# One written order for the whole first half: attention, W, a*b and c of batch 0

## The chip, the cores and the metric

The kernel runs on one core of a Trainium2 chip. The metric is the time of one execution on the device in microseconds (us). TensorE (PE) does the matmuls, ScalarE (ACT) and VectorE (DVE) read PSUM and do elementwise work, GpSimd (POOL) does elementwise work from SBUF to SBUF, and SyncE (SP) issues every DMA. Each of these engines works through its own list of instructions in order.

## The reference, cut to what matters

Attention over 16 heads of 576 tokens (two batches of eight heads), then two feed-forward parts:

```
scores = q @ k^T / 8, causal; a = softmax(scores); local = a @ v
q_p = phi(q); mem_out = (q_p @ M_prev) / (q_p @ z_prev + 1e-6)
attn = g * mem_out + (1 - g) * local          # g from beta, per head

x = attn, heads side by side                  # 1152 tokens x 512
h = (x @ w1) * (x @ w2) @ w3;  x = h @ w_out  # w3: 1024x1024, w_out: 1024x512
p = probs / sum(probs)
out = sum over 4 experts e of p[:, e] * (relu(x @ ew1[e]) @ ew2[e])
```

The weights `w1`, `w2`, `w3`, `w_out` arrive as 64-bit floats.

## The kernel before, in words

Heads are worked on in eight pairs: 0 to 3 are batch 0, 4 to 7 batch 1. Each matrix is split into a rounded high part and a low remainder, and a product is three matmuls (`PASSES`): high by low, low by high, high by high.

The first half of the program has four kinds of work:

- **Attention**, pair by pair. The parts are named by letters, a pair number and sometimes a step: `hq`, `hk`, `lq`, `lk` split q and k; `e`, `f` make phi; `s` scores (PE), `m` mask and row minimum (DVE), `x` exponential (ACT); `t` transposes (PE) and `c` their copies (ACT); `n`, `g` the memory read; `v` probabilities by v (PE), `j` and `ja` join the results (DVE, POOL); `z`, `zh`, `zl` write the transposed result `xT` (PE, ACT, DVE).
- **W = w3 @ w_out**, formed once, in 16 units of `u`: `wa` (ACT) and `wd` (DVE) turn a tile of 64-bit numbers into 32-bit ones, `wp` splits it on POOL, `w{u}_0` to `w{u}_3` are 12 matmuls into a bank `wacc`, and `y` takes the sum out: units 0 to 7 into `half` by ACT, units 8 to 15 added to `half` on DVE as `both`, which is then split into `W`. The eight tiles of `w_out` come by `oa`, `od`, `oh`, `ol` into `wo`.
- **a*b of batch 0**: 16 units, alternately of w1 and w2. Each is loaded, turned (ACT, DVE), written back to DRAM as `wf` for batch 1, split on POOL into `ws`, and gives two products `ab` of 12 matmuls. The products of the even unit are copied (`asb`, ACT), those of the odd one multiplied into it (DVE), and the result is split into `hT` (ACT, DVE).
- **c of batch 0** = W by hT: eight banks of 24 matmuls, each copied out by ACT into `x2`.

After these come a*b and c of batch 1 and the expert stage, about 462 us of the span.

A list of names, `FIRST`, states the order of PE, ACT, DVE and POOL for pairs 0 to 3 and units 0 to 6 of W, inside a `manual_schedule` block. Everything behind it is placed by rules: `run_slot` merges the steps of one pair with a share of `fill` work by fractions (`A_AT`, `T_AT` and so on; W's units in slot 4, a*b in slots 5 and 6, c in slot 7), and the Tile scheduler then decides the order of the instructions on each engine. SP's order is decided by the scheduler throughout.

Raw weight tiles are loaded ahead through `staging`: the first `RING` loads go to four slots in `main`, those behind them to two slots of the tag `raw`, where a load waits until the join two loads earlier has read its slot (`ahead`, `fetch`). In `FIRST` these loads are of `wo` and `w3`; a*b's loads have code of their own in `BUnits`.

Of the kernel before, what the change touches and what calls it, by code (L numbers as in the profile page):

```python
# [8 lines left out]
F32 = mybir.dt.float32  # L9
# [37 lines left out]
def kernel(  # L47
# [117 lines left out]
    def load_pair(p):  # L165

        ts = []
        for nm, src in (("q", qT), ("k", kT)):
            t = A2.tile([P, src.shape[-1]], F32, tag=f"{nm}d", name=f"{nm}d{p}")
            nc.sync.dma_start(out=t, in_=src[p])  # L170
            ts.append(t)
        raw_t[p] = ts
# [7 lines left out]
    def named(fs, ats):  # L180
        parts.update(fs)
        return [*zip(ats, fs.values())]

    def stage_h(p):

        if p >= B * H // 2:
            return []
        qd, kd = raw_t[p]

        def split(i):  # L190
            if p not in qk_t:
                qk_t[p] = [A1.tile([P, 2, w], F32R, tag=f"{x}s", name=f"{x}s{p}") for x, w in (("q", S + SB), ("k", S))]
            return (qk_t[p][i], (qd[:, 0 : S + SB], kd)[i])
# [8 lines left out]

        return named({f"hq{p}": lambda: hi(0), f"hk{p}": lambda: hi(1), f"lq{p}": lambda: lo(0), f"lk{p}": lambda: lo(1)}, H_AT)

    def stage_phi(p):

        if p >= B * H // 2:
            return []
        qd = raw_t[p][0][:, P:]
        st = {}  # L210

        def f0():
            st["ex"] = ex = A1.tile([P, S], F32, tag="ex", name=f"ex{p}")
            nc.scalar.activation(ex, qd, AF.Exp)

        def f1():
# [3 lines left out]
            nc.vector.scalar_tensor_tensor(out=phi, in0=qd, scalar=0.0, in1=ex, op0=ALU.max, op1=ALU.add)  # L220

        return named({f"e{p}": f0, f"f{p}": f1}, PHI_AT)

    def stage_a(p):

        if p >= B * H // 2:
            return []
        banks = {}
        prob_t[p] = Pt = {}
        mn = A2.tile([P, NS2 + 1], F32, tag="mn", name=f"mn{p}")  # L230
# [48 lines left out]
        return [(at, lambda c=c: (scores(*c), peaks(c))) for at, c in zip(A_AT, steps)]  # L279
# [13 lines left out]
    def stage_b(p):  # L293
# [5 lines left out]
        def trans(g):  # L299
# [16 lines left out]
            return lambda: (f(), copy())  # L316
# [85 lines left out]
        def fin_lo():  # L402
# [6 lines left out]
        return [  # L409
            *zip(T_AT, (trans(g) for g in range(len(GROUPS)))),  # L410
            (MEM_AT, lambda: (mem(), mem_out())), (PV_AT[0], pv(0)), (PV_AT[1], lambda: (pv(1)(), pv_last())),
            (JOIN_AT, lambda: (join(), join_mem())), (FIN_AT, lambda: (fin(), fin_hi(), fin_lo())),
        ]

    def run_slot(n, fill):
        steps = stage_h(n + 2) + stage_phi(n + 1) + stage_a(n + 1)
        steps += stage_b(n) if n >= 0 else []
        steps += [((i + 0.5) / len(fill), f) for i, f in enumerate(fill)]
        for _, f in sorted(steps, key=lambda t: t[0]):
            f()  # L420

# [21 lines left out]
    def wo_unit(c):  # L443
# [22 lines left out]
    def w_conv(u):  # L466
# [14 lines left out]
        fs = {f"wa{u}": acts, f"wd{u}": join, f"wp{u}": split}  # L481
        parts.update(fs)
        return lambda: [f() for f in fs.values()]

    def w_mm(u, c):
# [8 lines left out]
        if c == 3 and u >= W_FIRST:  # L494
            w_out_of(u)

    def w_out_of(u):
        g, t = divmod(u, KF)
        if g == 0:
            nc.scalar.copy(half[t], wacc[u])  # L500
        else:
            both = pf.tile([P, DM], F32, tag="asb", name=f"both{t}", bufs=1)
# [5 lines left out]
    def w_unit(u):  # L508
        def post():
            if u + 2 < NU:  # L510
                w_conv(u + 2)()

        return [lambda c=c: w_mm(u, c) for c in range(4)] + [post]

# [5 lines left out]
    class BUnits:  # L520


        def __init__(self, b, hi, lo):
            self.b, self.pool, self.hi, self.lo, self.ahead = b, pf, hi, lo, 2 + 2 * b
            self.raw, self.ws, self.asb = {}, {}, {}

        def load(self, u):
# [7 lines left out]
            self.raw[u] = r = self.pool.tile([P, KD, P, 2], U32, tag="raw", name=f"wr{self.b}_{u}")  # L535
# [15 lines left out]
        def mm(self, u, a):  # L551
            b = self.b
            m, w = divmod(u, 2)
            ps = psM.tile([P, 512], F32, tag=f"M{a}", name=f"ab{b}_{u}_{a}", bufs=1)
# [8 lines left out]
            if w == 0:  # L563
                if a == 0:
# [514 lines left out]
```

## Time and profile before

| | us |
|---|---|
| median of 3 runs | 720.12 (718.15 to 721.86) |
| the profiled execution's own time | 721.79 |
| its span, first to last instruction | 720.0 |
| PE busy | 691.7 (96%) |
| DVE busy | 423.6 (59%) |
| ACT busy | 375.7 (52%) |
| POOL busy | 368.5 (51%) |

Busy time of PE holds the time of matmuls that overlap, and a matmul is shown longer than its share of the stream. So a busy PE is not yet a PE at its best pace; that is read from chains of matmuls that follow each other without a wait. The span was profiled once; the profiled execution took 1.8 us more than its span.

### The profile page before, as it was taken

How to read it: one execution, taken by the hardware profiler on the slowest of the kernel's cores; microseconds unless marked ns; L12 is line 12 of the kernel's file. 1: busy time of each engine (PE TensorE's matmuls, PEld its weight loads, DVE VectorE, ACT ScalarE, POOL GpSimd, SP SyncE). 2: the span in 40 equal slices, each digit the busy share in tenths (PEclk: the TensorE clock that was granted, in tenths of full speed). 3: DMA queues.
4: the chain of work that ended last, by engine and by line, in shares of the span. 5: the costliest groups of instructions: out<-in, count | busy, mean ns of one | idle time of the engine just before them, and what ended most of it. 6: DMA issues, size and time to landing. Idle time of an engine off the chain costs nothing.

```text
span 720.0 us, 12876 instructions
## 1 busy us (share of the span) xinstructions
PE 691.7 (96%) x4952; PEld 616.7 (86%) x4952; DVE 423.6 (59%) x785; ACT 375.7 (52%) x793; POOL 368.5 (51%) x357
## 2 busy tenths in 40 slices
PE   4889998989999999999999999999999999999997
PEld 3667775779899999999898999889999989998896
DVE  6698899877743133335866565346554455634563
ACT  6879967465733143336454554454554455444441
POOL 3435546637341050002776776566866577766660
PEclk9999999999999999999999999999999999999999
DMA  8663333354530022102212331313231313221511
GB/s 285 229 196 127 99 116 117 120 193 150 176 133 30 9 100 69 60 17 71 90 59 66 111 118 59 117 59 104 73 117 59 117 60 117 91 86 59 188 31 59
DMA packets 43404, 74.53 MB, mean 104 GB/s; under 512 B 14416, under 2 KB 14416, under 8 KB 43344
## 3 DMA queue, kind: packets, MB, share of 16 engines
q1 hardware_dynamic: 43344, 73.72, 30.7%
q8 instruction: 39, 0.64, 0.4%
q14 instruction: 21, 0.17, 0.1%
HBM read 67.15 MB, written 6.55 MB: 102 GB/s over the span
## 4 chain that ended last, share of the span: by engine, by line
PE 77%; DVE 10%; ACT 4%; DMA 4%; POOL 2%; issue 2%; SPq 0%; DVEq 0%; ACTq 0%
PE o L905 27%; PE Z L952 14%; PE ab L558 11%; PE Q L952 7%; PE c L665 6%; PE R L952 3%; PE a L331 2%; PE wacc L490 2%; PE pt L307 2%; PE sc L252 1%; DMA qd<-in_q_cols_dram 1%; DMA wr<-in_moe_w_tiles_dram 1%; PE sc L240 1%; DVE tf_l L126 1%; DMA wor<-in_moe_w_out_dram 1%
## 5 line engine op out<-in xcount | busy, mean ns | idle before, releaser
L905 PE MATMUL o<-w,he 128*128 128x512 f32 x864 | 224.0, 392 | 0.0
L93 POOL TENSOR_TENSOR w<-r,w 128x512 fp32r<-128x512 f32 x96 | 129.8, 1352 | 165.1 <-ACT w L786 159.8
L905 PEld LDWEIGHTS o<-w,he 128*128 128x128 f32 x864 | 153.7, 188 | 23.8
L558 PE MATMUL ab<-xT,ws 128*128 128x288 f32 x768 | 111.1, 298 | 3.4 <-DVE asb L652 1.9
L558 PEld LDWEIGHTS ab<-xT,ws 128*128 128x128 f32 x768 | 103.4, 188 | 6.5 <-issue 2.0
L890 ACT ACTIVATE he<-t 128x320 fp32r<-128x320 f32 (+1 forms) x96 | 42.7, 445 | 118.3 <-DVE t L981 70.5
L891 DVE SCALAR_TENSOR_TENSOR he<-t,he 128x320 fp32r<-128x320 f32 (+1 forms) x96 | 57.8, 602 | 49.1 <-ACT he L890 49.1
L96 DVE TENSOR_TENSOR w<-r,w 128x512 fp32r<-128x512 f32 x64 | 66.7, 1044 | 0.0
L974 DVE TENSOR_TENSOR t<-u,Q 128x320 f32<-128x320 f32 (+1 forms) x32 | 14.5, 454 | 82.4 <-ACT u L972 82.4
L786 ACT CAST w<-r 128x512 fp32r<-128x512 f32 x96 | 58.9, 614 | 4.4 <-POOL r L799 2.6
L490 PE MATMUL wacc<-wo,w3s 128*128 128x512 f32 x192 | 54.1, 419 | 3.1 <-DVE both L503 2.7
L665 PE MATMUL c<-hT,W 128*128 128x288 f32 (+2 forms) x384 | 53.9, 296 | 0.0
L665 PEld LDWEIGHTS c<-hT,W 128*128 128x128 f32 x384 | 51.7, 188 | 0.3
L952 PE MATMUL Z<-X0T,w 128*128 128x320 f32 x288 | 50.3, 310 | 0.1
L952 PEld LDWEIGHTS Z<-X0T,w 128*128 128x128 f32 x288 | 46.1, 188 | 4.1 <-ACT u L968 0.6
L490 PEld LDWEIGHTS wacc<-wo,w3s 128*128 128x128 f32 x192 | 35.2, 195 | 12.9 <-issue 5.1
L952 PEld LDWEIGHTS Z<-X1T,w 128*128 128x128 f32 x288 | 41.0, 188 | 4.0
L952 PE MATMUL Z<-X1T,w 128*128 128x256 f32 x288 | 42.1, 282 | 0.0
L816 ACT CAST w<-r 128x512 fp32r<-128x512 f32 x64 | 39.5, 618 | 0.0
L266 DVE CUSTOM_DVE_ANT_0 P<-sc,mask 128x128 f32<-128x128 f32 (+4 forms) x72 | 33.7, 513 | 8.6 <-PE sc L240 5.7
L271 ACT ACTIVATE P<-P,mn 128x128 f32<-128x128 f32 (+4 forms) x72 | 37.5, 582 | 2.2 <-DVE mn L266 2.2
L793 POOL TENSOR_TENSOR t<-r 128x256 f32<-128x256 f32 x32 | 32.1, 1003 | 7.9 <-DMA r<-in_moe_w_tiles_dram 7.9
(131 smaller groups left out, 1175.9 us busy)
## 6 DMA issues: line engine op xcount, KB each, us to landing
r<-in_moe_w_tiles_dram SPq DMA_DIRECT2D x64, 256.0 KB, 3.7
r<-in_moe_w_dram SPq DMA_DIRECT2D x64, 256.0 KB, 2.9
w3r<-in_moe_w_tiles_dram SPq DMA_DIRECT2D x16, 512.0 KB, 3.9
wr<-in_moe_w_tiles_dram SPq DMA_DIRECT2D x16, 512.0 KB, 3.6
wor<-in_moe_w_out_dram SPq DMA_DIRECT2D x8, 512.0 KB, 5.5
wf<-tf SPq DMA_DIRECT2D x16, 256.0 KB, 2.1
wr<-wf SPq DMA_DIRECT2D x16, 256.0 KB, 2.8
qd<-in_q_cols_dram SPq DMA_DIRECT2D x8, 352.0 KB, 3.1
```

Of the source, the lines that this page charges most:

```text
L93: nc.gpsimd.tensor_sub(dst, src, r32(hi))
L96: nc.vector.tensor_sub(dst, src, r32(hi))
L271: nc.scalar.activation(Pt[i, x], Pt[i, x], AF.Exp, bias=one, scale=-1.0)
L490: nc.tensor.matmul(wacc[u], lhsT=w3s[u][:, a, c, :], rhs=wo[4 * g + c][:, bb, :], start=(c == 0 and x == 0), stop=(c == 3 and x == 2),)
L558: nc.tensor.matmul(ps[:, 0:HS], lhsT=self.ws[u][:, wi, kk, :], rhs=xT[b, kk][:, xi, a * HS : (a + 1) * HS], start=(n == 0), stop=(n == 3 * ...
L665: nc.tensor.matmul(st["ps"], lhsT=Wt[kk][:, wi, d * P : (d + 1) * P], rhs=hT[kk][:, xi, t0 : t0 + tw], start=(kk == 0 and x == 0), stop=(k ...
L786: return lambda: nc.scalar.copy(st["w"][i][:, 0], src(i))
L816: return lambda: nc.scalar.copy(w2s[s][x][:, 0], st["r"][:, x])
L890: nc.scalar.activation(h[:, 0], src, AF.Relu)
L891: nc.vector.scalar_tensor_tensor(out=h[:, 1], in0=src, scalar=0.0, in1=r32(h[:, 0]), op0=ALU.max, op1=ALU.subtract)
L905: nc.tensor.matmul(o_ps[i], lhsT=h_of[s][x][:, a, i * P : (i + 1) * P], rhs=w2s[s][x][:, b, :], start=first, stop=last,)
L952: nc.tensor.matmul(ps, lhsT=w1s[s][a][:, wi, kk, :], rhs=X[c, b][:, xi, kk, :], start=first and kk == 0 and x == 0, stop=(kk == 1 and x == ...
```

## The change: what it does

`FIRST` now holds 720 names and states the order for all eight pairs, all of W, a*b of batch 0 and c of batch 0, in one `manual_schedule` block. `run_slot`, the fractions, `spread` and `fills` are gone. The functions that made several steps at once (`w_unit`, `w_out_of`, `emit`, `BUnits.unit` for batch 0) are cut into named parts, so that each can be placed. a*b's loads of batch 0 go through `staging` and the same chain of loads as `wo` and `w3`, `RING` is 12 instead of 17, and q and k of a pair are loaded apart. W's units 7 to 15 stood in pair 4's slot; in the list, a*b's units 0 to 7 come between W's first half and its second, and units 8 to 15 behind W. The number of matmuls and of elementwise instructions stays as it was. Batch 1 and the expert stage are written as before and are still placed by the scheduler.

```diff
-FIRST_PAIRS, W_FIRST, RING = 4, 7, 17
-W_SLOTS, B_SLOTS, C_SLOTS = (4.0, 5.0), (5.0, 7.0), (7.0, 8.0)
+zl3 s40 y4 s41 wp6 oa4 m40 w5_0 w5_1 m41 x40 w5_2 od4 w5_3 x41 w6_0 wp7 y5 w6_1 ba0 w6_2 w6_3 oh4 bd0 w7_0 y6 w7_1 ol4
...
+b5_1 rm20 bp6 rh20 v51 rm21 rh21 rl20 b6_0 bd7 rl21 wa8 b6_1 bp7 bc60 v52 head14 head15 bc61 wd8 b7_0 j5 wa9 wp8 b7_1
...
+RING = 12
-    def load_pair(p):
...
+    def load(nm, p):
+        src = {"q": qT, "k": kT}[nm]
+        raw_t[nm, p] = t = A2.tile([P, src.shape[-1]], F32, tag=f"{nm}d", name=f"{nm}d{p}")
+        nc.sync.dma_start(out=t, in_=src[p])
...
-    def run_slot(n, fill):
...
-        if c == 3 and u >= W_FIRST:
-            w_out_of(u)
...
+    def w_sum(u):
+        def add():
+            if g == 0:
+                nc.scalar.copy(half[t], wacc[u])
+                return
+            st["f"] = both = pf.tile([P, DM], F32, tag="asb", name=f"both{t}", bufs=1)
             nc.vector.tensor_add(both, half[t], wacc[u])
+        def hi():
             Wt[t] = main.tile([P, 2, DM], F32R, tag=f"u{t}", name=f"W{t}")
-            nc.scalar.copy(Wt[t][:, 0, :], both)
-            lo_dve(Wt[t][:, 1, :], both, Wt[t][:, 0, :])
+            nc.scalar.copy(Wt[t][:, 0, :], st["f"])
...
-            self.raw[u] = r = self.pool.tile([P, KD, P, 2], U32, tag="raw", name=f"wr{self.b}_{u}")
+            self.raw[u] = r = staging(f"wr{self.b}_{u}")
...
+        def acts(self, u):
+            self.raw[u] = from64_acts(self.raw[u], self.pool, f"0_{u}")
+        def join(self, u):
+            self.raw[u] = f = from64_join(*self.raw[u])
+            wf[u] = wd.tile([P, KD, P], F32, tag=f"f{u}", name=f"wf{u}")
+            nc.sync.dma_start(out=wf[u], in_=f)
+            ahead()
...
+        def keep(self, u, a):
+            nc.scalar.copy(self.asb[m][:, a, :], self.ps[u, a][:, 0:HS])
+        def times(self, m, a):
+            nc.vector.tensor_mul(pa_, self.ps[2 * m + 1, a][:, 0:HS], pa_)
+        def h_hi(self, m, a):
+            nc.scalar.copy(hT[m][:, 0, a * HS : (a + 1) * HS], self.asb[m][:, a, :])
+        def h_lo(self, m, a):
+            lo_dve(hT[m][:, 1, sl], self.asb[m][:, a, :], hT[m][:, 0, sl])
...
-    order = [f for f in FIRST if f[:2] in ("oa", "wa")]
-    order += [f"wa{u}" for u in range(W_FIRST + 2, NU)]
+    order = [f for f in FIRST if f[:2] in ("oa", "wa", "ba")]
...
-    fills = spread(W_SLOTS, [w_unit(u) for u in range(W_FIRST, NU)])
-    fills += [(B_SLOTS[0], [b0_start])] + spread(B_SLOTS, [b0.unit(u) for u in range(NU)])
-    fills += [(7.5, [b1.start])]
-    fills += spread(C_SLOTS, [c_unit(0, d, a * HS, HS, ps_main(d, a)) for d in range(KD) for a in range(2)])
...
+    with tc.manual_schedule(engines=ENGINES):
+        for f in FIRST:
+            parts[f]()
+    b1.start()
```

In the new list `ba`, `bd`, `bp` are acts, join and split of a unit of a*b, `b{u}_0` and `b{u}_1` its products, `bc` the copy, `rm`, `rh`, `rl` the product and its split, `k` and `kc` the matmuls and copies of c.

On PE, this is where W's second half begins before, beside pair 4 (`sc_5` are scores of pair 5, `pt_4` transposes of pair 4; the numbers behind the last `_` only tell tiles apart):

```order
L490 MATMUL wacc_1481<-wo_123,w3s_1389 128x512 x3
L490 MATMUL wacc_1481<-wo_124,w3s_1389 128x512 x3
L490 MATMUL wacc_1481<-wo_125,w3s_1389 128x512 x3
L252 MATMUL sc_5_1438<-ks_1254,qs_1253 128x128 x6
L252 MATMUL sc_5_1438<-ks_1254,qs_1253 128x256 x5
L490 MATMUL wacc_1406<-wo_126,w3s_1322 128x512 x3
L252 MATMUL sc_5_1438<-ks_1254,qs_1253 128x256
L307 MATMUL pt_4_1485<-identF,P_8_1273 64x128
L252 MATMUL sc_5_1492<-ks_1254,qs_1253 128x384 x6
L490 MATMUL wacc_1481<-wo_126,w3s_1389 128x512 x3
```

Units 8 (`wacc_1406`) and 9 (`wacc_1481`) stand in pieces between each other and between single matmuls of the scores. After the change PE's list reads there, with `ab_7` unit 7 of a*b and `sc_6` the scores of pair 6:

```order
L536 MATMUL ab_7_1_2044<-xT_3_74,ws_7_1995 128x288 x3
L467 MATMUL wacc_2064<-wo_123,w3s_2041 128x512 x3
L467 MATMUL wacc_2064<-wo_124,w3s_2041 128x512 x3
L467 MATMUL wacc_2064<-wo_125,w3s_2041 128x512 x3
L467 MATMUL wacc_2064<-wo_126,w3s_2041 128x512 x3
L244 MATMUL sc_6_2087<-ks_1724,qs_1723 128x384 x6
L244 MATMUL sc_6_2094<-ks_1724,qs_1723 128x512 x6
L467 MATMUL wacc_2105<-wo_123,w3s_2076 128x512 x3
```

Units, products and score steps stand whole, and unit 8 has moved behind a*b's unit 7.

On DVE, this is what stands ahead of the first addition of W's second half (`both`) before; `ex_2209` and `ex_2756` are phi of pairs 6 and 7, `tf_l` the joins of later w3 tiles:

```order
L219 TENSOR_SCALAR ex_2209<-ex_2209 128x576
L126 SCALAR_TENSOR_TENSOR tf_l_1470<-tf_l_1470,tu_l_1471 128x512
L127 SCALAR_TENSOR_TENSOR tf_l_1470<-w3r_1216,tf_l_1470 128x512
L220 SCALAR_TENSOR_TENSOR phi_2251<-qd_1341,ex_2209 128x576
L126 SCALAR_TENSOR_TENSOR tf_l_1516<-tf_l_1516,tu_l_1517 128x512
L219 TENSOR_SCALAR ex_2756<-ex_2756 128x576
L127 SCALAR_TENSOR_TENSOR tf_l_1516<-w3r_1387,tf_l_1516 128x512
L126 SCALAR_TENSOR_TENSOR tf_l_1589<-tf_l_1589,tu_l_1590 128x512
L127 SCALAR_TENSOR_TENSOR tf_l_1589<-w3r_1476,tf_l_1589 128x512
L503 TENSOR_TENSOR both_1433<-half_63,wacc_1406 128x512
```

After the change the addition of the same unit stands between two mask steps of pair 6 (`P_12`, `P_13`; `mn` rows read their minimum), behind one w3 join and the last a*b rows:

```order
L134 SCALAR_TENSOR_TENSOR tf_l_2079<-tf_l_2079,tu_l_2080 128x512
L135 SCALAR_TENSOR_TENSOR tf_l_2079<-w3r_2015,tf_l_2079 128x512
L105 TENSOR_TENSOR hT_3_2058<-asb_3_1998,hT_3_2058 128x288
L260 ISA P_12_2117,mn_1836<-sc_6_2094,mask 128x512
L260 ISA P_13_2119,mn_1836<-sc_6_2094,mask 128x512
L481 TENSOR_TENSOR both_2130<-half_63,wacc_2064 128x512
L260 ISA P_12_2134,mn_1836<-sc_6_2087,mask 128x384
L260 ISA P_13_2136,mn_1836<-sc_6_2087,mask 128x384
```

No phi of later pairs and no more than one w3 join stand directly ahead of it.

## Rows read from the trace of the kernel before

**Rows 1.** Busy us of each engine by stretch; clock, DMA.
```profile
0.00:80.00 80.00, 64.78 (x661) 50.25 (x663) 62.83 (x159) 64.80 (x126) 34.04 (x38) 0.98 0.62 203
80.00:258.00 178.00, 171.20 (x1512) 148.84 (x1511) 117.27 (x235) 95.85 (x188) 78.36 (x68) 0.99 0.34 114
75.00:136.00 61.00, 56.78 (x475) 43.98 (x475) 53.84 (x107) 43.15 (x80) 33.26 (x27) 0.97 0.32 104
100.00:120.00 20.00, 15.86 (x92) 10.62 (x92) 18.68 (x41) 14.55 (x28) 7.68 (x7) 0.91 0.35 123
258.00:270.00 12.00, 10.93 (x81) 10.50 (x80) 6.00 (x8) 5.73 (x13) 6.21 (x6) 1.00 0.23 74
```
**Rows 2.** PE's waits, 80 to 270 us: total, times, longest.
```profile
PE wacc L490 <- DVE both L503: 2.7, 1, 2.7
```
**Rows 3.** The chain that ended last, 94 to 120 us: start, us, what.
```profile
96.05 4.46 DMA qd<-in_q_cols_dram
...
112.32 0.61 DVE both L503
...
115.42 3.99 PE wacc L490 x11
```
**Rows 4.** The chain, 76 to 90 us, where PE never waits.
```profile
76.79 0.72 PE sc L252 x6
...
78.52 1.37 PE wacc L490 x6
79.89 1.32 PE a L331 x40
81.21 0.91 PE sc L252 x6
...
84.33 0.88 PE a L341 x20
85.20 1.00 PE sc L240 x6
...
87.58 0.87 PE pt L307 x8
88.45 0.90 PE b L365 x8
89.34 0.29 PE b L369 x4
```
**Rows 5.** The chain, 188 to 250 us: products of a*b, transposes back.
```profile
188.39 1.58 PE ab L558 x12
190.95 1.79 PE ab L558 x12
...
249.59 0.44 PE x L392 x4
250.03 0.29 PE x L397 x4
```
**Rows 6.** Busy us of c's matmuls alone, 80 to 258 us: PE, PEld, ACT.
```profile
80.00:258.00 178.00, 26.27 (x191) 25.50 (x192) 2.79 (x7) 0.99 0.34 114
```
**Rows 7.** Groups by line: a*b's turning, then w3's join at 75 to 136 us.
```profile
L119 ACT ACTIVATE tu<-wr 128x512 uint32<-128x512 uint16 x14 | 9.5, 679 | 17.0 <-DMA wr<-in_moe_w_tiles_dram 15.9 <-DVE mn L266 0.6 <-DVE tf L126 0.3
L126 DVE SCALAR_TENSOR_TENSOR tf<-tf,tu 128x512 uint32<-128x512 uint32 x16 | 13.9, 871 | 7.6 <-ACT tf L120 7.2
L126 DVE SCALAR_TENSOR_TENSOR tf_l<-tf_l,tu_l 128x512 uint32<-128x512 uint32 x9 | 9.1, 1010 | 1.0 <-ACT tu_l L119 1.0
```
**Rows 8.** DMA issues: size, median us to landing.
```profile
wr<-in_moe_w_tiles_dram SPq DMA_DIRECT2D x16, 512.0 KB, 3.6
mz<-in_m_z_dram SPq DMA_DIRECT2D x1, 520.0 KB, 8.4
```
**Rows 9.** DVE in order of time: two like joins, the first beside a POOL split.
```profile
102.52 1.63 DVE L126 SCALAR_TENSOR_TENSOR tf_l<-tf_l,tu_l 128x512 uint32<-128x512 uint32 x1 [0.75 <-ACT tu_l L119]
...
107.55 0.68 DVE L126 SCALAR_TENSOR_TENSOR tf_l<-tf_l,tu_l 128x512 uint32<-128x512 uint32 x1
```

More of the change, by code (lines that the diff above doesn't have):

```diff
@@ L408, in stage_b @@
         })
[L409 to L413, printed above, removed]
-    def run_slot(n, fill):
[L416 to L420, printed above, removed]
+        for g in range(len(GROUPS)):
+            trans(g)
     p2 = ExitStack()
@@ L479, in split @@
             lo_pool(w3s[u][:, 1], st["f"], w3s[u][:, 0])
-        fs = {f"wa{u}": acts, f"wd{u}": join, f"wp{u}": split}
-        parts.update(fs)
-        return lambda: [f() for f in fs.values()]
+        parts.update({f"wa{u}": acts, f"wd{u}": join, f"wp{u}": split})
     def w_mm(u, c):
@@ L493, in w_mm @@
             )
-        if c == 3 and u >= W_FIRST:
-            w_out_of(u)
-    def w_out_of(u):
+    def w_sum(u):
         g, t = divmod(u, KF)
[L499 to L502, printed above, removed]
+        st = {}
+        def add():
[3 more added lines that the diff above has]
+            st["f"] = both = pf.tile([P, DM], F32, tag="asb", name=f"both{t}", bufs=1)
             nc.vector.tensor_add(both, half[t], wacc[u])
+        def hi():
             Wt[t] = main.tile([P, 2, DM], F32R, tag=f"u{t}", name=f"W{t}")
-            nc.scalar.copy(Wt[t][:, 0, :], both)
-            lo_dve(Wt[t][:, 1, :], both, Wt[t][:, 0, :])
[L508 to L513, printed above, removed]
+            nc.scalar.copy(Wt[t][:, 0, :], st["f"])
+        parts.update({
+            f"y{u}": add, f"yh{u}": hi, f"yl{u}": lambda: lo_dve(Wt[t][:, 1, :], st["f"], Wt[t][:, 0, :]),
+        })
     hT = {}
@@ L597, in fetch @@
         if i < len(order):
-            (wo_load if order[i][0] == "o" else w_load)(int(order[i][2:]))
+            loads[order[i][0]](int(order[i][2:]))
     def ahead():
@@ L609 @@
     fetch(0), fetch(1), fetch(2)
-    load_pair(1)
+    load("q", 1), load("k", 1)
     fetch(3)
@@ L668, in f, with out @@
                         )
-                if k1 == KF:
-                    nc.scalar.copy(x2[b][d // 2][:, d % 2, t0 : t0 + tw], st["ps"])
-            return f
-        return [mm(k, k + 2) for k in range(0, KF, 2)]
+            return f
+        def out():
+            if b not in x2:
+                x2[b] = [main.tile([P, 2, S], F32, tag=f"g{2 * b + k}", name=f"x2_{b}{k}") for k in range(2)]
+            nc.scalar.copy(x2[b][d // 2][:, d % 2, t0 : t0 + tw], st["ps"])
+        return [mm(k, k + 2) for k in range(0, KF, 2)] + [out]
@@ L691, with define @@
-    fills += [(7.5, [b1.start])]
-    fills += spread(C_SLOTS, [c_unit(0, d, a * HS, HS, ps_main(d, a)) for d in range(KD) for a in range(2)])
-    for n in range(FIRST_PAIRS, B * H // 2):
-        if n + 2 < B * H // 2:
-            load_pair(n + 2)
-        if n > FIRST_PAIRS and 2 * n + 3 < B * H:
-            load_head(2 * n + 2), load_head(2 * n + 3)
-        run_slot(n, sum([f for at, f in fills if n <= at < n + 1], []))
+    def define(p):
+        stage_h(p), stage_phi(p), stage_a(p), stage_b(p)
@@ new lines @@
+    NPAIR = B * H // 2
+    for p in range(NPAIR):
+        define(p)
+        parts.update({f"load{nm}{p}": lambda nm=nm, p=p: load(nm, p) for nm in "qk"})
+        parts.update({f"head{n}": lambda n=n: load_head(n) for n in (2 * p, 2 * p + 1)})
+    for c in range(KF):
+        wo_unit(c)
+    for u in range(NU):
+        w_conv(u), w_sum(u)
+        parts.update({f"w{u}_{k}": lambda u=u, k=k: w_mm(u, k) for k in range(4)})
+        parts.update({
+            f"ba{u}": lambda u=u: b0.acts(u), f"bd{u}": lambda u=u: b0.join(u), f"bp{u}": lambda u=u: b0.conv(u),
+        })
+        for a in range(2):
+            parts[f"b{u}_{a}"] = lambda u=u, a=a: b0.product(u, a)
+            if u % 2 == 0:
+                parts[f"bc{u}{a}"] = lambda u=u, a=a: b0.keep(u, a)
@@ new lines @@
+    for a in range(2):
+        for m in range(KF):
+            for nm, f in (("rm", b0.times), ("rh", b0.h_hi), ("rl", b0.h_lo)):
+                parts[f"{nm}{m}{a}"] = lambda f=f, m=m, a=a: f(m, a)
+        for d in range(KD):
+            fs = c_unit(0, d, a * HS, HS, ps_main(d, a))
+            parts.update({f"k{d}{a}_{q}": f for q, f in enumerate(fs[:4])})
+            parts[f"kc{d}{a}"] = fs[4]
+    with tc.manual_schedule(engines=ENGINES):
+        for f in FIRST:
+            parts[f]()
```

167 lines of the change are left out of this document (62 added, 105 removed).

## The prediction

> **What bounds the kernel now.** I read the busy time by stretch first. Batch 0 ends at 258 us, where the products of batch 1 begin; what lies behind that, 462 us, is written as before. Ahead of it there are two regimes [rows 1]. In the first 80 us DVE and ACT are each busy 63 to 65 us, and PE's 64.8 us contain long overlaps and waits: the attention of the first pairs and the turning of 64-bit weights feed PE too slowly. From 80 to 258 us PE is busy 171.2 of 178 us, DVE only 117.3 and ACT 95.9. A stated order can gain in the second regime what PE waits there and what it loses to small pieces, and in the first only what DVE and ACT lose.
>
> Next, PE's waits behind 80 us. The longest single one is 2.7 us for `both` on DVE [rows 2]. The chain shows what made it [rows 3]: a load of q for a later pair (4.46 us, from 96.05), on whose landing ACT's exponential hung, then joins of later w3 tiles on DVE, and `both`, done at 112.9 us. The order printed above shows the same, since phi of pairs 6 and 7 and four joins stand ahead of the addition. The wait costs twice: in the stretch from 100 to 120 us the granted clock averages 0.91, so part of it ran at the lower level of 1.2 GHz [rows 1], and right behind the wait eleven W matmuls take 3.99 us, 363 ns each [rows 3], against 228 ns at full pace [rows 4].
>
> **The change, step by step.** No work is removed. So I ask where PE stands at a common point, and what is left for it there.
>
> *First part.* In the old run 159 DVE instructions have started by 80 us [rows 1]. In the new order DVE's 157th row belongs to `j3`, just ahead of `w3_0` (the first part of W's unit 3). Up to there the list holds all scores, transposes and probabilities-by-v of pairs 0 to 3, 13 parts of W (39 matmuls) and eleven joins: 703 matmul records by my count, against 661 in the old 80 us. The kinds of work on DVE are nearly the same (one more `g` and `j` and two more `f`, two fewer joins). At DVE's old share, 62.8 of 80 us, this point comes at about 80 us again. Lower bound: if DVE reaches the 53.8 of 61 us that it shows from 75 to 136 us [rows 1], 71 us. Upper: ACT has to do as much, and one more load in its way costs a landing of 3.6 us [rows 8], 84 us. I take 79, near the old pace, because the start, the loads and the early list are alike.
>
> *What is left for PE then.* Prices come from the chain from 76 to 90 us, where PE never waits and the switches between kinds of work are contained [rows 4]; this was a stretch with whole steps, as the new list has them.
> - W: 51 parts of three matmuls. Two parts take 1.37 us; a unit of four, with about 0.2 us for entering it (a transposes step of eight takes 0.87 us there, 0.11 each, so such a switch is no more), 2.94 us. 51/4 x 2.94 = 37.5 us.
> - a*b: 32 products. They take 1.58 or 1.79 us in the chain [rows 5]; at 1.68 this is 53.8 us.
> - c: 192 matmuls, 26.3 us [rows 6].
> - Attention, pairs 4 to 7. Scores: 0.72 for the 128- and 256-wide ones (as many columns as the row of six), 0.72, 0.91, 1.00; transposes 25/8 x 0.87 = 2.72; v 1.32 twice and 0.88; memory read 0.90 + 0.29 [rows 4]; z 0.44 + 0.29 [rows 5]. Together 11.5 us a pair, 46.0 for four, and `z3` 0.7.
>
> The sum is 164.3 us, against the 178 us that the old run needed from 80 us on. A cross-check: 1,437 matmul records are left, against 1,512 [rows 1]; at the old pace by records they take 169 us, waits included, a bound from above if the mix were the same. From below, products at 1.58 throughout and no entering cost give 158.5.
>
> *Waits in the second part.* With the list at hand I followed it from unit 7 of a*b to the end. A unit of W's second half needs from DVE a join of two passes at 1.01 us [rows 7], 0.6 for `both` [rows 3] and one more pass for W's low part, 3.6 us by these means against PE's 2.9; but between the units stand scores, transposes, the memory read and `v` of pair 6, and DVE can run ahead during a*b's units 6 and 7. I find no wait over 1 us there. Late in the list two things are tight. Pair 7's `z6` and `n7` need a score bank that DVE frees with its masks: 1.0 us. And a*b's loads: with two slots, the load of unit i+2 can only be issued when unit i is joined, so two units cannot be closer than landing 3.6, two ACT passes of 0.68 each and two DVE passes of 0.87 [rows 7, 8], 6.7 us, and about 0.5 for SP, which first issues the `wf` write. That is 7.2 us for two units of 6.7 us on PE: 0.5 us in each of the last three rounds, 1.5 us. In the old run this same round is seen as 15.9 us of ACT waiting for `wr` [rows 7]; it costs nothing as long as other work stands between the units, and the new list spreads eight of them over pairs 4 and 5. Waits together: 2.5 us.
>
> So batch 0 ends at 79 + 164.3 + 2.5 = 245.8 us instead of 258.0: 12.2 us less.
>
> *The joint with batch 1.* From 258 to 270 us PE is idle for 1.07 us [rows 1], waiting for ACT, which first does a cast of the expert weights. In the new ACT order the second copy of `asb` stands ahead of that cast; the product that follows needs only the copy. I take 1.0 us. Bounds: nothing, or 2 us lost, since pair 7's `z7` now ends some 2 us nearer to the joint and the expert loads start behind it.
>
> Behind that nothing moves. The profiled execution took 721.79 us for its span of 720.0; less 13.2 it is 708.6, and the median of the runs, 1.67 lower, becomes **706.9**, so 707.
>
> **The port that DVE and POOL share.** A join beside a POOL split took 1.63 us, the same join alone 0.68 us [rows 9]; over W's stage it averages 1,010 ns, over all of a*b 871 ns [rows 7]. The Trainium skill, SBUF — State Buffer, section "Who interferes with whom", has it that a DVE instruction with two SBUF inputs and a GpSimd one that reads SBUF exclude each other for a whole instruction; the trace agrees, with 1.63 against 0.68. This speaks against the change, which packs the same splits into fewer us. By the old means the sum stands. At the W stage's mean instead, the joins behind the cut (30, two passes each) cost DVE 60 x 0.14 = 8.4 us more. DVE then has some 124 us to do before c's 26 us, where PE needs 138; at the best share seen, 0.88, it takes 141, and batch 0 ends 3 us later: 710.
>
> **The rivals.**
> - *DVE stays the bound (no change).* Behind the cut DVE has 117.3 us of work [rows 1], nearly all ahead of c, where PE has 138 us: it must be busy 0.84 of the time. From 75 to 136 us it reached 0.88, in the first 80 us 0.79 [rows 1]. In one fixed order on four engines each waits for the others' latest. If DVE gets only 0.76, a*b ends at 79 + 153, c at 258: about 719 to 720. For it: the list has no scheduler to fill holes. Against it: in the second part the list has PE-heavy work between DVE-heavy work.
> - *The loads become the bound (slower).* Twenty-six loads, of `wo`, w3 and w1/w2, go through two slots in thirteen rounds; SP is one queue, and what stands behind a load that waits (q, k, v, `wf`) waits with it. At 7.2 us the rounds need 94 us of the 150 that there are. From 11.3 us a round there is no gain left; with the slowest landing of this size, 8.4 us [rows 8], a round is 12 us, 156 together, and c ends near 267: 729. Against it: the median landing of `wr` is 3.6 us, and 8.4 is a single load's.
> - *More than counted (faster still).* DVE keeps 0.88 from the start: the cut at 71 to 74 us, no further waits: 699 to 701.
>
> **Numbers.** Runs of this kernel lie 0.3% around their median, so half a per cent, 3.6 us, is what can be told from no change: faster is below 716.5, slower above 723.7. Chances: the forecast 0.48 (702 to 712), the shared port as priced 0.10 (708 to 714), more than counted 0.16 (696 to 702), DVE the bound 0.16 (714 to 723, all but 0.03 of it no change), loads or another blocked queue 0.10 (724 to 730). Faster 0.77, same 0.13, slower 0.10. The range leaves out the slower case, about half of the DVE case's upper part and the last of the fast one: 697 to 720.
>
> **What would show it.** In the new profile batch 1's first product should begin near 246 us; the place of `w3_0` near 79 us; from there PE should never wait over 1.5 us; W's second half should take 2.9 us a unit without a drop of the clock; the last six units of a*b should be 3.4 to 3.7 us apart. The forecast is wrong if DVE's busy share between the cut and c is below 0.8, if ACT waits for `wr` or `w3r` show up as waits of PE, if PE enters the cut later than 84 us, or if the 462 us behind the joint change by more than 2 us.

## The result, and the profile after

The changed kernel takes 703.34 us (median of four runs, 702.97 to 703.90). The kernel before, run beside it, takes 720.99 us. The ratio is 0.9762, 95% interval [0.9731, 0.9793]: faster by 17.6 us by the medians, and by 15 to 19 us by the interval. The forecast was 707 us, in a range of 697 to 720.

The profiled execution took 703.90 us, its span is 702.2. First the page's busy times, then stretches in the columns of [rows 1] (PE, PEld, DVE, ACT, POOL, granted clock, DMA share, GB/s).

```profile
span 702.2 us, 12869 instructions
...
PE 680.7 (97%) x4952; PEld 613.7 (87%) x4952; DVE 416.0 (59%) x785; ACT 376.0 (54%) x793; POOL 364.5 (52%) x357
```

```profile
0.00:74.70 74.70, 61.88 (x731) 49.81 (x732) 58.20 (x156) 60.38 (x116) 30.80 (x35) 1.00 0.61 191
74.70:239.70 165.00, 163.35 (x1438) 146.41 (x1438) 113.92 (x236) 99.61 (x196) 75.68 (x69) 1.00 0.41 135
100.00:120.00 20.00, 18.90 (x218) 16.84 (x217) 16.79 (x40) 15.37 (x33) 10.37 (x9) 1.00 0.61 195
240.00:260.00 20.00, 18.19 (x136) 17.96 (x135) 9.70 (x14) 8.88 (x21) 8.15 (x8) 1.00 0.21 67
```

The first row ends at the cut, where `w3_0` is done (74.7 us); the second ends where batch 1's first product begins (239.7 us, 258.2 before). In the second stretch PE is busy 163.35 of 165.0 us, and its clock stays at the full level; from 100 to 120 us PE was busy 15.86 us at a mean granted clock of 0.91 before [rows 1], and is now busy 18.90 us at 1.00.

PE's waits in the first 260 us (total, times, longest):

```profile
PE sc L244 <- DVE ks L105: 7.3, 1, 7.3
PE sc L244 <- DVE mn L260: 2.9, 3, 2.4
PE ab L536 <- DVE asb L550: 1.8, 1, 1.8
PE ab L536 <- ACT asb L546: 0.9, 1, 0.9
```

The first two are the start (the wait for the first load, and one of 2.4 us in pair 0). Behind 15 us nothing is over 0.9 us until the joint with batch 1, where PE waits 1.8. The 2.7 us for `both` [rows 2] are gone, and so is what stood behind them [rows 3]. The chain through W's second half now consists of PE alone (start, us, what), with 2.73 to 3.00 us for the twelve matmuls of a unit:

```profile
140.61 2.73 PE wacc L467 x12
143.34 1.42 PE sc L244 x12
144.76 3.00 PE wacc L467 x12
147.76 0.79 PE sc L232 x6
148.54 2.77 PE wacc L467 x12
```

To compare kernels in which the same work stands in another order, I gave each PE instruction the time that it takes when nothing hinders it (230 ns for a W matmul, 133 for one of a*b or c, 109 for a transpose, and so on, from chains like this one) and added them up in the order of the trace. These sums are estimates, good to about 1 us. The table shows when each kernel has done the same sum. It is used for the experiments too (times in us).

| full-pace work done | before | after | newhead | oldhead | oldhead2 | wfirst2 | late_both |
|---|---|---|---|---|---|---|---|
| 20 | 43.1 | 39.0 | 38.9 | 41.5 | 41.6 | 39.0 | 39.1 |
| 60 | 91.3 | 86.9 | 87.7 | 91.2 | 91.3 | 92.0 | 87.0 |
| 70 | 102.0 | 97.4 | 102.8 | 112.9 | 105.2 | 109.6 | 97.6 |
| 80 | 120.7 | 109.5 | 116.2 | 123.9 | 118.5 | 120.9 | 109.2 |
| 120 | 169.1 | 153.9 | 170.6 | 170.4 | 162.7 | 174.7 | 161.5 |
| 210 | 268.4 | 250.5 | 271.1 | 267.9 | 258.8 | 272.3 | 258.1 |
| batch 1's first product | 258.2 | 239.7 | 261.1 | 256.5 | 248.1 | 261.8 | 247.2 |

Between before and after 4.4 us are won by 60, another 6.6 between 70 and 80 (the wait for `both`, the slow clock behind it and a few smaller waits around it), and 6.7 in small steps from there to 210. From batch 1's first product to the end there are 462.5 us, against 461.9.

### The profile page after: what moved, and what is told of

It reads as the page before. It is cut to its first block, busy times and chain, and to the rows that moved or that the text cites. A ratio compares the mean times of both kernels' runs of the same rounds, so it can differ in the third digit from the quotient of the medians.

```text
span 702.2 us, 12869 instructions
## 1 busy us (share of the span) xinstructions
PE 680.7 (97%) x4952; PEld 613.7 (87%) x4952; DVE 416.0 (59%) x785; ACT 376.0 (54%) x793; POOL 364.5 (52%) x357
## 4 chain that ended last, share of the span: by engine, by line
PE 83%; DVE 7%; DMA 3%; ACT 3%; issue 2%; POOL 1%; SPq 0%; DVEq 0%; ACTq 0%; POOLq 0%
PE o L882 27%; PE Z L929 14%; PE ab L536 12%; PE Q L929 7%; PE c L628 7%; PE wacc L467 4%; PE R L929 4%; PE a L323 2%; PE pt L300 2%; DVE P L260 2%; PE sc L244 1%; DMA wor<-in_moe_w_out_dram 1%; DMA w3r<-in_moe_w_tiles_dram 1%; PE a L333 1%; ACT pT L304 1%
## 5 line engine op out<-in xcount | busy, mean ns | idle before, releaser
L102 POOL TENSOR_TENSOR w<-r,w 128x512 fp32r<-128x512 f32 x96 | 130.2, 1356 | 169.1 <-ACT w L763 163.8
L536 PE MATMUL ab<-xT,ws 128*128 128x288 f32 x768 | 107.9, 297 | 2.8 <-DVE asb L550 1.8
L467 PE MATMUL wacc<-wo,w3s 128*128 128x512 f32 x192 | 48.6, 400 | 0.5 <-DVE wo L105 0.5
L304 ACT COPY pT<-pt 128x512 f32<-128x512 f32 (+1 forms) x56 | 28.3, 541 | 10.3 <-PE pt L300 10.0
```

The lines of the kernel that those rows point to most:

```text
L102: nc.gpsimd.tensor_sub(dst, src, r32(hi))
L467: nc.tensor.matmul(wacc[u], lhsT=w3s[u][:, a, c, :], rhs=wo[4 * g + c][:, bb, :], start=(c == 0 and x == 0), stop=(c == 3 and x == 2),)
L536: nc.tensor.matmul(ps[:, 0:HS], lhsT=self.ws[u][:, wi, kk, :], rhs=xT[b, kk][:, xi, a * HS : (a + 1) * HS], start=(n == 0), stop=(n == 3 * ...
```

## The experiments

### The two halves of the list apart: newhead, oldhead, oldhead2, oldhead3

**newhead** is the kernel before, with its own list put into the order that the new list has.

```diff
-hq0 e0 lq0 hk0 lk0 oa0 s00 f0 load2 od0 s01 m00 wa0 m01 s02 oh0 x00 ol0 wd0 s03 x01 m02 wp0 oa1 ...
+hq0 e0 lq0 hk0 lk0 load2 wa0 f0 s00 wd0 s01 m00 oa0 wp0 m01 s02 x00 od0 s03 x01 m02 hq1 t00 t02 ...
```

> The kernel before, with the 296 names of its old list put in the order in which the new list has them; the rules that place all the rest stay. Theory: the order of the early list alone is worth 4 to 6 us, since the cut at w3_0 comes 5.5 us earlier in the changed kernel at the same DVE share; the wait for both, and the pieces behind it, stay: 715 to 717 us. Rival A, the early gain comes with the loads (RING of 12, q and k loaded apart) and not with the order: 720 to 721. Rival B, the early order only moves work behind the list, where the rules' part then takes longer: the cut is early, and the time is 719 to 722.

It took 723.75 us, 1.0025 of before [1.0009, 1.0041]. Rival B holds in kind, though the time lies above its 719 to 722: 3.6 us are won by 60 in the table, and by 210 it has lost 6.3 again. The early gain comes with `RING` at 17 and with q and k loaded together, so rival A is out; how much of it is clock is seen at oldhead3. Behind the list W's second half follows at once, for which the new order has kept back the last four tiles of `w_out`; DVE, from 100 to 140 us, has little room (busy 0.89, then 0.97):

```profile
100.00:120.00 20.00, 15.85 (x181) 12.29 (x181) 17.76 (x41) 16.55 (x33) 9.81 (x8) 1.00 0.20 54
120.00:140.00 20.00, 18.87 (x108) 13.46 (x108) 19.44 (x37) 13.45 (x25) 12.19 (x11) 1.00 0.37 123
```

**oldhead** is the changed kernel with the old list's names first, in their old order, then the rest of the new list.

```diff
+... y5 wp7 w6_1 f4 oa7 w6_2 ja3 w6_3 od7 y6 wp8 z3 zh3 oh7 zl3 ol7
+e5 loadq6 f5 loadk6 e6 ba0 bd0 w7_0 w7_1 w7_2 bp0 w7_3 y7 b0_0 b0_1 ...
-RING = 12
+RING = 17
```

> The changed kernel, with the 296 names of the old list first, in their old order, then what is left of the new list; RING is 17 as before. Theory: it loses the early gain and keeps the rest, since behind the old list no phi and no joins stand ahead of both: 707 to 709 us, and no wait of PE over 1.5 us between the list's end and the joint. Rival A, the early order is worth nothing: 703 to 704. Rival B, the second part's pace rests on what the new early list has left ready (joined tiles of w_out late, a*b early): over 711, with new waits right behind the old list.

It took 720.68 us, 0.9995 [0.9972, 1.0017]: nothing is left of the gain; the theory's 707 to 709 was wrong, and rival B (over 711, with new waits right behind the old list) is right. The chain shows what the joint of the two lists costs:

```profile
99.49 0.77 DVE phi L215
...
100.32 2.51 DMA qd<-in_q_cols_dram
102.83 0.69 DVE tf L135
...
104.37 1.59 POOL ws L102
...
106.00 4.93 PE ab L536 x23
```

It is the same thing as before's wait for `both`: phi and a load of q stand ahead of the join that PE's next work needs. PE waits 6.0 us for the split, the clock averages 0.83 from 100 to 120 us, and between 60 and 70 in the table 21.7 us go by, against 10.5. Besides, the old list splits w3's ninth tile early (`wp8`), and that tile then keeps one of the two `ws` slots through eight units of a*b.

**oldhead2** puts these back, and **oldhead3** also moves `z3`.

The lines are those of oldhead and oldhead2:

```diff
-... y5 wp7 w6_1 f4 oa7 w6_2 ja3 w6_3 od7 y6 wp8 z3 zh3 oh7 zl3 ol7 e5 loadq6 f5 loadk6 e6 ba0 bd0 w7_0 ...
+... y5 wp7 w6_1 f4 oa7 w6_2 ja3 w6_3 ba0 od7 y6 bd0 z3 w7_0 zh3 w7_1 oh7 bp0 w7_2 zl3 ol7 w7_3 y7 ba1 b0_0 ...
```

> Old early list ahead of the new rest, as in oldhead, but without what made oldhead wait 6.0 us for ws: the early conversion and split of w3's ninth tile (wa8, wd8, wp8), which kept one of the two ws slots through a*b's units 0 to 7, goes back to its place in the new list, phi of pairs 5 and 6 goes behind a*b's first products, and a*b's first two joins are woven into W's unit 7. Theory: the old early list then costs only its own 4 to 5 us: 707 to 709, with the same pace behind 100 us as in the changed kernel. Rival, the second part needs more than that from the new early list (ACT and DVE less far ahead): over 711, with PE waits over 2 us behind 95 us.

It took 712.58 us, 0.9879 [0.9855, 0.9902]: by its number the rival's case. But from 70 on in the table it keeps the changed kernel's pace (153.6 us from 70 to 210, against 153.1). What it lacks is 4.4 us by 60, the old list's own, and 3.4 from 60 to 70, where PE waits 1.6 us at `z3`; the twelve W matmuls behind that take 4.53 us, and the clock averages 0.91 from 80 to 100 us:

```profile
95.57 4.53 PE wacc L467 x12
```

> The list of oldhead2, with z3 behind two parts of W's unit 7 on PE instead of ahead of them. In oldhead2 PE stood 1.6 us at z3, behind a split and a join on POOL, and the twelve W matmuls after it took 4.5 us. Theory: that junction cost the 3.9 us that oldhead2 lost against the changed kernel beyond the old list's own 4.4; without it 707.5 to 709.5. Rival, the loss only moves to the next late input behind the old list (a*b's first split): 711 to 713.

It took 714.55 us (710.85 to 716.26), 0.9935 [0.9912, 0.9957]. The rival is right in kind (its 711 to 713 was still too low): the wait at `z3` is gone, one of 1.0 us for `ws` is new, one of 2.1 us ahead of transposes stays (2.0 in oldhead2), and now the clock averages 0.91 from 100 to 120 us. The profiled execution (710.85 us) was the quickest of its six, with a mean clock of 0.998 against 0.990 to 0.993 in the others. In it the clock did not fall in the first 80 us, and the old list then reaches 60 at 88.7 us instead of 91.3. So of the new list's 4.4 us, up to 2.6 are clock that the old list loses in some executions, and at least 1.8 the order itself.

### W's second half ahead of a*b: wfirst, wfirst2, wfirst_ring17

**wfirst** puts W's units 8 to 15 into the places of a*b's units 0 to 7, and these behind them. **wfirst2** has the same order, with the first joins of each kind woven into the last units of the kind before, and **wfirst_ring17** is wfirst2 with `RING = 17`. The lines are those of wfirst2.

```diff
-... w6_1 ba0 w6_2 w6_3 oh4 bd0 w7_0 y6 w7_1 ol4 oa5 w7_2 bp0 w7_3 s42 y7 od5 b0_0 m42 oh5 b0_1 ba1 ...
+... w6_1 oh7 ol7 w6_2 w6_3 wa8 w7_0 y6 wd8 w7_1 wa9 w7_2 wp8 w7_3 s42 y7 w8_0 m42 w8_1 wd9 x42 s43 ...
```

> The changed kernel, with the places of a*b's units 0 to 7 and W's units 8 to 15 exchanged: the last tiles of w_out first, then W's second half beside the attention of pairs 4 and 5, then a*b's units 0 to 7 beside pair 6. Every engine's work stays the same. Theory: a unit of W's second half asks 3.3 to 3.6 us of DVE against 2.9 of PE, and beside the scores of pairs 4 and 5, which ask DVE for masks and minima, PE waits for DVE: 706 to 711 us, with PE waits on both and w3s. Rival, the order of the two is indifferent, since DVE is busy only 0.69 of the second part: 702.5 to 704.5.

> W's second half ahead of a*b again, as in wfirst, but with each kind's first joins woven into the last units of the kind before, so that no switch from one kind to the other starts from an empty queue. Theory: W's second half beside the attention of pairs 4 and 5 is short of DVE (3.3 to 3.6 us of DVE a unit, plus masks), so PE waits from 90 to 130 us, with DVE over 0.9 busy there: 707 to 712. Rival A, only the badly woven switches cost in wfirst: 703 to 705. Rival B, the last four w_out tiles in the early part are what costs, because their joins stand beside the masks of pairs 2 to 4 and make the cut late: 706 to 712 too, but with the loss ahead of 90 us.

> The list of wfirst2 with RING 17. In wfirst2 ACT waited 3.4 us for a w_out tile at 83.6 us with the copy of W's unit behind it, and PE for that copy. Theory: it is the loads through two slots, with w_out's last four tiles wanted together with w3's, that cost the 12 us between 75 and 110 us; with 17 loads in the four slots of main most of them go: 711 to 716. Rival, the loads only hide that ACT, POOL and DVE have too much to turn and split in that stretch: 720 to 724.

They took 726.93 us (1.0067 of before [1.0046, 1.0088]), 724.43 (1.0044 [1.0023, 1.0064]) and 722.02 (1.0019 [0.9996, 1.0042]): all of the gain is lost, more than any theory for the first two said. By the medians weaving gave back 2.5 us and the ring 2.4, where the runs of each kernel spread over 4 to 7 us. Rival B of wfirst2 has a part in it: of the 21.8 us that wfirst2 is behind the changed kernel at 210 in the table, 5.1 are lost by 60, 7.1 from 60 to 70 and 9.6 behind. For wfirst_ring17 the rival (720 to 724) holds: the loads were only a part. Its stretch from 80 to 100 us:

```profile
80.00:100.00 20.00, 12.92 (x56) 9.13 (x54) 15.35 (x32) 14.68 (x28) 5.88 (x6) 0.91 0.12 44
```

PE is busy 12.9 us there (20.00 in the changed kernel), while DVE is busy 0.77 and not the 0.9 that I had expected. The chain goes back and forth between ACT's passes, DVE's joins and masks, and POOL's splits, each in its stated order, with twelve tiles (eight of w3, four of `w_out`) to be turned for 23.5 us of PE (eight units at the prediction's 2.94). I read this as a latency; DVE is not simply full. PE's longest waits from 75 to 165 us in wfirst_ring17 say the same, since they are for results of different engines:

```profile
PE sc L244 <- DVE xT L105: 3.4, 1, 3.4
PE pt L300 <- ACT pT L304: 2.7, 2, 2.3
```

The third is 2.2 us for ACT's copy `asb`. A W-first list woven better than mine was not tried, so these runs give the price of these lists and not of every such list.

### The price of a wait: late_both, late_short

The changed kernel, with the first addition of W's second half (`y8`) behind two joins, or behind one.

```diff
-w9_3 y8 x62 m61 s63 ja5 yh8 w10_0 m63 x61 w10_1 wd11 w10_2 hk7 hq7 w10_3 yl8 wa12 t60 wp11 y9 t61 z4 yh9 n6 c60 wd12
+w9_3 x62 m61 s63 ja5 w10_0 m63 x61 w10_1 wd11 w10_2 hk7 hq7 wa12 wd12 y8 yh8 yl8 w10_3 t60 wp11 y9 ...   (late_both)
+w9_3 x62 m61 s63 ja5 w10_0 m63 x61 w10_1 wd11 y8 yh8 w10_2 hk7 hq7 w10_3 yl8 wa12 t60 wp11 y9 ...   (late_short)
```

> The changed kernel, with the addition y8 (the first both) and its two splits placed behind the joins of W's units 11 and 12 on DVE, as before's order had such an addition behind four joins. Theory: PE stands 2 to 5 us behind w9, as long as DVE's two joins and ACT's two passes for the second of them need, nothing of it is won back because PE has no idle time left behind it, and the granted clock falls for some us behind the wait: 706 to 709 us. Rival A, the wait costs its own length and no more, the clock stays: the time rises by just the wait. Rival B, the other engines get ahead meanwhile and PE's later small waits vanish: under 704.5.

> As late_both, with the first addition behind one join only (wd11), so that the wait is shorter. Theory: DVE is free for the addition some 2.7 us later than PE wants it; the wait costs its length and, as in late_both (5.9 us, and 4.9 instead of 2.9 us for the twelve W matmuls behind it), 1.5 to 2 us more for matmuls at the lower clock: 707 to 708.5. Rival, a wait of this length leaves the clock alone: 705.5 to 706.3, with 2.7 to 3.0 us for the twelve matmuls behind it.

late_both took 712.15 us, 8.8 more than the changed kernel. PE waits 5.9 us; its wait, then the chain behind it:

```profile
PE wacc L467 <- DVE both L481: 5.9, 1, 5.9
...
153.31 0.61 DVE both L481
153.92 0.14 issue
154.06 4.88 PE wacc L467 x12
```

4.88 us for twelve matmuls that take 2.77 in the changed kernel: wait and slower clock together cost 8.0 us (by the same sums 18.9 us go by from 110 to 120, against 10.9), and nothing of it comes back: the kernel is 7.6 us behind the changed one at 120, and 7.6 at 210. late_short took 706.45 us, 3.1 more, with a wait of 2.9 us:

```profile
PE wacc L467 <- DVE both L481: 2.9, 1, 2.9
...
149.21 0.61 DVE both L481
149.82 0.14 issue
149.96 3.00 PE wacc L467 x12
```

Here the clock stayed up in the profiled execution. Of its four runs two took 705.0 and 705.8 us, at a mean clock of 1.000, and two 707.1 and 707.3, at 0.997 and 0.996. So the kernel loses no more than the wait's length where the clock stays, and some 1.5 to 2 us more where it falls; theory and rival each hold in half of the runs. That the clock fell right behind this wait in the two longer runs is not shown: the trace is of the run of 705.0 us.

### What was left: ring17, joint, best

**ring17** is the changed kernel with `RING = 17`. **joint** moves pair 7's end forward among c's products. **best** is both.

```diff
-k11_3 k20_0 kc11 v71 k20_1 t76 k20_2 c76 k20_3 v72 kc20 k21_0 j7 k21_1 k21_2 ja7 k21_3 k30_0 kc21 z7 k30_1 zh7 ...
+b15_1 v71 rm70 rh70 rl70 t76 k00_0 rm71 rh71 c76 k00_1 rl71 k00_2 v72 k00_3 j7 k01_0 kc00 ja7 k01_1 k01_2 k01_3 z7 ...
```

> The changed kernel with RING 17 as before, so that five more loads go through the four slots in main and are issued four joins ahead. Theory: the loads are not what bounds the changed kernel, except from 81 to 101 us, where ACT hung on two w_out loads and PE then waited 0.9 us: 702.3 to 703.3. Rival, the loads' rounds bind more than the waits show: under 702. Rival on the other side, the slots in main come free later for xT of pair 4: over 704.

> The changed kernel, with the end of pair 7 (v71, t76, c76, v72, j7, ja7, z7, zh7, zl7) some 12 us earlier among c's products. Theory: the 1.8 us wait at the joint hangs on the expert loads, which start when z7 has freed their slots; with z7 near 222 instead of 234 us the wait is gone: 701.0 to 702.2. Rival, PE then waits for pair 7's own steps (ACT's and DVE's results stand between c's first products) or for the same casts at another place: 703 to 704.5.

> The list of joint with RING 17. Theory: the two gains lie at places that don't touch (81 to 101 us and the joint) and add up, 2.3 and 0.5 us: 700.2 to 701.0. Rival, they overlap, or the smaller one was no gain: 701.0 to 702.0.

ring17 took 702.85 us, 0.5 less than the changed kernel, as expected; the runs of the two overlap (702.68 to 703.10, and 702.97 to 703.90), so the loads bind little or not at all. joint took 701.04, 2.3 less (five runs, 700.83 to 703.23; the profiled one was the longest, and its 1.8 us wait at the joint is gone all the same). In the changed kernel the chain at the joint runs from the end of `z7` over SP's issues and a load of expert weights to POOL and ACT, where a cast stands ahead of `hT`:

```profile
233.84 0.29 PE x L389 x4
...
235.58 4.22 DMA r<-in_moe_w_tiles_dram
...
246.92 0.03 ACT w L763
...
247.44 0.44 ACT hT L555
...
249.12 0.46 DVE asb L550
249.57 0.04 issue
249.62 1.87 PE ab L536 x12
```

In joint's chain `z7` ends at 221.8 us, and behind it there are only products:

```profile
221.50 0.27 PE x L389 x4
221.76 19.27 PE c L628 x144
241.03 9.01 PE ab L536 x68
```

best took 700.69 us, 0.9733 of before [0.9711, 0.9755]: better than both kernels by 20 and 2.7 us, close to the sum of its two parts (2.8).

## Why the prediction was right, and where its sizes were off

*First part.* I had the cut at 79 us; it came at 74.7. The forecast of DVE's share was right: 58.20 of 74.7 us, 0.78, as in the old first 80 us (0.785) [rows 1]. The step that failed is "the kinds of work on DVE are nearly the same": I counted 157 instructions against 159 and took equal numbers for equal time. By groups of lines, before (0 to 80 us) and after (0 to 74.7 us), the passes of the joins stood so:

```profile
L127 DVE SCALAR_TENSOR_TENSOR tf_wo<-wor,tf_wo 128x512 uint32<-128x512 uint32 x6 | 7.6, 1264 | 0.2
L127 DVE SCALAR_TENSOR_TENSOR tf_l<-w3r,tf_l 128x512 uint32<-128x512 uint32 x7 | 7.1, 1011 | 0.2
L126 DVE SCALAR_TENSOR_TENSOR tf_l<-tf_l,tu_l 128x512 uint32<-128x512 uint32 x7 | 6.7, 959 | 2.6 <-ACT tf_l L120 2.6
L126 DVE SCALAR_TENSOR_TENSOR tf_wo<-tf_wo,tu_wo 128x512 uint32<-128x512 uint32 x6 | 4.6, 774 | 1.8 <-ACT tf_wo L120 1.8
```

```profile
L135 DVE SCALAR_TENSOR_TENSOR tf_l<-w3r,tf_l 128x512 uint32<-128x512 uint32 x7 | 6.0, 850 | 0.2
L134 DVE SCALAR_TENSOR_TENSOR tf_l<-tf_l,tu_l 128x512 uint32<-128x512 uint32 x7 | 5.1, 725 | 1.8 <-ACT tf_l L128 1.8
L135 DVE SCALAR_TENSOR_TENSOR tf_wo<-wor,tf_wo 128x512 uint32<-128x512 uint32 x4 | 3.9, 968 | 0.1
L134 DVE SCALAR_TENSOR_TENSOR tf_wo<-tf_wo,tu_wo 128x512 uint32<-128x512 uint32 x4 | 2.7, 686 | 0.0
```

26.0 us for 26 passes became 17.7 us for 22: four fewer, and each 0.2 us shorter. Masks fell by 2.2 us, phi rose by 3.5, and the rest by 2.4. The sum is 4.6 us less work on DVE ahead of the cut; at the old share of 0.785, 58.20 us of work put the cut at 74.1.

This is an account by shares and does not show DVE to be the cause. The clock has a part as well: in the first 80 us it averages 0.98 before [rows 1] and 1.00 after, and oldhead3 has shown up to 2.6 us for that. I had not counted it. Why each pass became shorter was not tested. My count of matmuls was off too: 703 ahead of the cut by the list, 731 in the trace.

*What is left for PE, and its waits.* 164.3 + 2.5 = 166.8 us were forecast, 165.0 measured. PE is busy 163.35 us of these, so about half of the 1.8 us is work that was priced too high (164.3) and half is waits: 1.65 us idle, where I had 2.5, 1.0 for pair 7's score bank and 1.5 for the round of the loads. Neither of the two shows up as a wait of PE; the longest one there is 0.9 us, for ACT's copy `asb`, which two loads of `w_out` had held up. The last six units of a*b begin 3.2 to 5.2 us apart, with pair 7's steps between them (I had said 3.4 to 3.7), so the round of 7.2 us for two units never bound; ACT waits 5.3 us for `wr`, against 15.9 before [rows 7]. ring17 agrees from the other side, with 0.5 us. DVE is busy 109.0 of the 136.0 us between cut and c, 0.80, where I had 0.84 and took less than 0.8 as a sign against the forecast.

*The joint.* I had 1.0 us won there; 0.6 were lost (462.5 us behind it, against 461.9), and PE's wait there, 1.8 us, is over the 1.5 that I had allowed. The bound "2 us lost, since `z7` ends nearer to the joint and the expert loads start behind it" was the right mechanism, as the chain and joint show, and the value taken was the wrong one.

The sum, against 13.2 forecast: 4.3 more from the first part, 1.8 more from the second, 1.6 less at the joint, 17.7 in all; the spans differ by 17.8. The joint's loss hid 1.6 of the 6.1 us by which the first two terms were off.

*The wait for both.* The prediction had its cost right in kind: PE stands, then runs at the lower clock. The stretch from 70 to 80 in the table is 6.6 us shorter, and late_both, which puts a longer wait back (5.9 us against 2.7), loses 8.0. (Of the four joins ahead of the addition the order printed for before shows three; the trace has the fourth, at 99.8 us, ahead of its first line.)

*What carries the gain.* The prediction took the second part as bound by PE and asked of DVE only whether it would keep up. The experiments say more: that part is bound by PE in this list, with a*b's first units ahead of W's second half, and in none of the three lists with W first. From 80 to 162 us the kernel before does 64.2 us of full-pace PE work, newhead 59.0, the three W-first lists 57 to 61, oldhead2 69.7 and the changed kernel 74.0; DVE is busy 70.6 us in before and 69.0 in the changed kernel, so the same DVE time carries more of PE's work. The order of the two kinds is not enough by itself: oldhead has a*b first too, and with its wait of 6.0 us it does only some 62. Why a*b first is better is argued and not shown. The groups of DVE in the changed kernel, 74 to 212 us, speak for one reason:

```profile
L134 DVE SCALAR_TENSOR_TENSOR tf<-tf,tu 128x512 uint32<-128x512 uint32 x16 | 13.4, 837 | 2.2 <-ACT tf L128 2.2
L135 DVE SCALAR_TENSOR_TENSOR tf<-wr,tf 128x512 uint32<-128x512 uint32 x16 | 12.2, 762 | 0.6
L134 DVE SCALAR_TENSOR_TENSOR tf_l<-tf_l,tu_l 128x512 uint32<-128x512 uint32 x9 | 11.5, 1281 | 4.1 <-ACT tf_l L128 4.1
L105 DVE TENSOR_TENSOR hT<-asb,hT 128x288 fp32r<-128x288 f32 x15 | 9.4, 634 | 3.8 <-ACT hT L555 3.8
L550 DVE TENSOR_TENSOR asb<-ab,asb 128x288 f32<-128x288 f32 x16 | 7.3, 454 | 4.9 <-PE ab L536 2.9 <-ACT tf L128 1.2 <-ACT tf_l L128 0.8
L135 DVE SCALAR_TENSOR_TENSOR tf_l<-w3r,tf_l 128x512 uint32<-128x512 uint32 x9 | 6.5, 724 | 0.3
L105 DVE TENSOR_TENSOR W<-both,W 128x512 fp32r<-128x512 f32 x8 | 5.7, 716 | 0.7 <-ACT W L485 0.7
L481 DVE TENSOR_TENSOR both<-half,wacc 128x512 f32<-128x512 f32 x8 | 5.5, 685 | 0.3
```

A unit of W's second half asks 1.28 + 0.72 + 0.72 + 0.69 = 3.4 us of DVE for 2.7 to 3.0 of PE, and the four `w_out` tiles come on top; a unit of a*b asks 0.84 + 0.76 and, as the mean of its two kinds of unit, 0.63 + 0.45, together 2.7 us for 3.2 to 3.4 of PE. Beside attention, which needs DVE for masks, the kind that is light on DVE would be the one that fits. Against this as the whole reason, DVE is busy only 59 to 63 of the 82 us in the W-first lists, and of PE's 12.5 to 13.1 us of idle time there from 75 to 165 us (1.5 in the changed kernel) at most 0.4 us are for `both`; most of the rest hangs on ACT's results, POOL's splits and `xT`. So the steps of a unit that wait for each other on three engines are a rival reason. Nor did a run keep before's broken-up units in another order, so what whole units alone are worth is open. The Trainium skill, Perfetto Trace Analysis, section "Optimization Strategy", says that a kernel whose most-contended engine changes over time may gain by interleaving such regimes; the trace agrees, with 74.0 us of PE's work in 82 us against 64.2 by the sums above.

*The rivals.* DVE as the bound (719 to 720) is nearest to what newhead became, with DVE busy 0.97 from 120 to 140 us. The loads as the bound did not come, as ring17 shows. "More than counted" named the early cut, but by a DVE share of 0.88 that was never reached. The shared port was priced at 3 us lost, for 30 joins behind the cut, where there are 29. The Trainium skill, SBUF — State Buffer, "Who interferes with whom", says that a DVE instruction with two SBUF inputs contends with a GpSimd one that reads SBUF. Single joins agree again (1.64 us for the second pass of one in late_both, beside a POOL split, and 0.69 for that of the one before it, with POOL idle), but DVE's busy time fell from 423.6 to 416.0 us, so the closer packing did not make DVE's work longer as a whole.

## What to carry to other kernels

The gain did not come in separable parts: either half of the list, put into the other's surroundings, gave 0 us or less at first, because each leaves things ready, or not ready, for the other; so a move is tested together with what follows it. When PE is to be the bound, try beside each other the kinds of work whose demands on the helping engine add up to less than PE's time, and price that demand in us by kind, never by number of instructions (156 of DVE's rows took 4.6 us less than 159 others). And look first at the one long wait: late_both paid its 5.9 us in full, with matmuls at the lower clock behind it, and nothing gave it back.

## What the runs showed of the hardware

- The runs of some kernels differ by the granted clock. Of fourteen runs of the kernel before, those at a mean clock of 0.997 or 0.998 took 718.6 to 720.7 us, and those at 0.992 or 0.993 took 722.7 to 723.3; the changed kernel, with no wait over 0.9 us between start and joint, stays within 1 us at 0.999 to 1.000. It is no rule: newhead's two runs at 0.998 took 722.0 and 724.2 us, joint's five at 0.999 to 1.000 lie 2.4 us apart, and oldhead2's four, with waits of 1.5 to 2.0 us, only 0.7.
- The lower clock behind a wait is no function of that wait's length alone in these runs: 5.9 us (late_both) was followed by twelve W matmuls in 4.88 us, 1.6 us (oldhead2) by twelve in 4.53, but 2.9 us (late_short) by twelve in 3.00.
